# Last weights of a decode attention kernel: one head a transfer on eight semaphores, and VectorE copies the half that is finished last

## Chip, cores and metric

The kernel runs on one core of one Trainium2 chip. The metric is the device time of one execution in microseconds (us). Executions of one kernel agree within some 0.3%. Times in the profile count from the span's start. The span (439.6 us before) is shorter than the time (441.3 us), because it runs from the core's first to its last instruction.

TensorE multiplies matrices (PE, and PEld for its weight loads), VectorE is DVE, ScalarE is ACT, GpSimd is POOL, and SyncE (SP) issues nearly all DMA transfers. Engines and transfers tell each other that they are done through semaphores, counters that one raises and another waits for.

## The reference

Two attention blocks with one new token per sequence, 4 sequences, 32 query heads on 8 key/value heads of width 128. Block A attends to all 8192 cached positions, block B to the last 2048. The two results are concatenated.

```python
q = (x @ wq).reshape(B, 1, 32, 128).transpose(0, 2, 1, 3)
scores = einsum("bhqd,bhkd->bhqk", q, repeat(k_cache, 4, axis=1)) * 128 ** -0.5
p = softmax(scores)
o = einsum("bhqk,bhkd->bhqd", p, repeat(v_cache, 4, axis=1))
return o.transpose(0, 2, 1, 3).reshape(B, 1, 4096) @ wo      # block A; B the same on k, v[..., -2048:, :]
# ... out = concatenate([a, b], axis=-1)
```

## The kernel before

K and V stream through SBUF, the core's on-chip memory, in 20 units. A unit is one sequence and two K/V heads of block A (4 MB of K, 4 MB of V), or one sequence of block B. TensorE transposes K, computes scores, sums the softmax and multiplies P by V. Ten turns of two units each run as a hardware loop on TensorE. The last unit, L, ends in straight code after the loop. Its output is projected with the last 8 heads of `wo`, which have a buffer of their own, `Wl_sb` (1 MB).

```python
# TensorE, after the loop. V of unit L comes in pieces of 4, 2, 1 and 1 eighths ("VL" 0..3).
VCH = [4, 2, 1, 1]
for c in range(NC):                                  # 8 chunks of 16 P.V matmuls
    w = [("VL", vch_of[c])]
    # ...
    if c == 4:
        pe_SM(L)                                     # softmax sum: 16 matmuls of 64 columns
        op("pe", pe_seed, waits=[("ocp", NTURN - 1)])  # puts the sum so far into both halves
    pe_PV(L, c, bank=KTB[0], waits=w)
add_norm(L, bank=KTB[0])                             # VectorE scales P.V by 1/sum: OT_sb ("otr")

WCH = [3, 2, 2, 1]                                   # heads per weights transfer
for i, n in enumerate(WCH):
    for hq in range(h0, h0 + n):
        for hf in range(2):                          # halves[0] in bank SA, halves[1] in bank KT
            # matmul(out=halves[hf], lhsT=OT_sb[..., hq, :], rhs=Wl_sb[:, hq, half hf])
            op("pe", lfn, waits=[("WL", i), ("otr", L), ("oc", L - 1)],
               inc=("fin", hf) if hq == C - 1 else None)
    h0 += n
op("dve", copy halves[0] to osb, waits=[("fin", 0)], inc=("ocp", NTURN))      # cut to its core
op("act", copy halves[1] to osb, waits=[("fin", 1)], inc=("Ef",))             # cut to its core
op("act", dma(out[:, 0, H2:D], osb[:, 0, H2:D]), waits=[("Ef",)], inc=("out", 2))

# SP, behind V of unit L:
for i, n in enumerate(WCH):
    src = WO[0][last 8 heads].rearrange("(h p) n -> p h n", p=128)[:, h0:h0 + n, :]
    op("sp", dma(Wl_sb[:, h0:h0 + n, :], src), inc=("WL", i))
    h0 += n
op("sp", dma(out[:, 0, 0:H2], osb[:, 0, 0:H2]), waits=[("ocp", NTURN)], inc=("out", 0))
# SP's end:
for i in range(3):
    sem, val, _ = values[("out", i)]
    sp.wait_ge(sem, val)
```

## Time and profile before

| | |
|---|---|
| time, 3 runs before the prediction | 441.33 us (441.18 to 441.64) |
| span of the profiled run | 439.58 us |
| DMA over the span | 420 GB/s |
| last piece of V lands | 433.90 us |
| last projection matmul starts | 437.08 us |
| last output lands, span ends | 439.08 us, 439.58 us |

The page of the kernel before: busy time of the engines, then two rows of 40 slices of the span (TensorE's granted clock in tenths, mean busy share of the 16 DMA engines in tenths).

```profile
PE 366.2 (83%) x7312; PEld 338.0 (77%) x7312; DVE 210.1 (48%) x462; ACT 186.4 (42%) x184; POOL 27.8 (6%) x84
PEclk9999999999999988998899799969997999899999
DMA  8999999999999999999999999999999999999995
```

The DMA row says 9 everywhere except at the two ends: the loads bound the kernel. The granted clock is 0.96 in the mean (one slice shows 0.6), and TensorE, busy for 83% of the span, has some slack. A change to the last transfers can move only the last few microseconds.

The chain of work that ended last, cut to its end (start, us, what):

```profile
411.39 23.49 DMA Wl_sb<-in_A_wo_dram
...
434.88 0.04 issue
...
435.42 0.36 issue
...
437.39 0.37 ACT osb L708
```

The chain comes through the first weights transfer, waits 0.36 us for nothing that the profile shows in the middle of the projection, and leaves through ScalarE's copy. The same stretch as a timeline (start, us, engine, line, operation; in brackets the idle time before it; in the timelines here the rows of weight loads (PEld) are left out, except where one is read):

```profile
434.62 0.18 DVE L489 TENSOR_TENSOR OT_sb<-KT,RL 128x8 bf16<-128x8 f32 x1 [2.29 <-PE KT L325]
434.93 0.08 PEld L703 LDWEIGHTS SA<-Wl_sb,OT_sb 128*4 128x4 bf16 x1 [0.46 <-DMA Wl_sb<-in_A_wo_dram]
434.93 0.27 PE L703 MATMUL SA<-Wl_sb,OT_sb 128*4 128x256 bf16 x1 [0.34 <-DMA Wl_sb<-in_A_wo_dram]
435.04 0.27 PE L703 MATMUL KT<-Wl_sb,OT_sb 128*4 128x256 bf16 x1
435.14 0.27 PE L703 MATMUL SA<-Wl_sb,OT_sb 128*4 128x256 bf16 x1
435.77 0.27 PE L703 MATMUL KT<-Wl_sb,OT_sb 128*4 128x256 bf16 x1 [0.36 <-issue]
...
437.08 0.27 PE L703 MATMUL KT<-Wl_sb,OT_sb 128*4 128x256 bf16 x1
437.28 0.41 DVE L707 CAST osb<-SA 4x256 bf16<-4x256 f32 x1 [2.48 <-PE SA L703]
437.39 0.37 ACT L708 ACTIVATE osb<-KT 4x256 bf16<-4x256 f32 x1 [10.84 <-PE KT L703]
437.72 0.29 SPq L567 DMA_DIRECT2D out_dram<-osb  x1
437.79 0.27 ACTq L567 DMA_DIRECT2D out_dram<-osb  x1
```

L489 is the scaling, L703 the projection. Matmuls follow each other 0.11 us apart, but the fourth starts 0.63 us after the third. This gap is called the stop below. The weights transfers by size (KB each, median us from issue to landing):

```profile
Wl_sb<-in_A_wo_dram SPq DMA_DIRECT2D x2, 256.0 KB, 23.7
Wl_sb<-in_A_wo_dram SPq DMA_DIRECT2D x1, 384.0 KB, 23.5
Wl_sb<-in_A_wo_dram SPq DMA_DIRECT2D x1, 128.0 KB, 9.9
```

The landing of each transfer, read from the semaphore records of the trace: V's last piece 433.90; weights 434.88, 435.51, 436.19 and 436.51. A transfer is shared by 16 engines, and it has landed when the slowest has finished: of the last piece of V, the first engine's share landed at 431.07, the second-last at 433.31, the last at 433.90.

### The profile page before, as it was taken

Reading aid. Unit: us, or ns where it says so; the run is one execution under the profiler, and the core shown is the slowest. Engines: PE = TensorE matmul, PEld = TensorE weight load, DVE = VectorE, ACT = ScalarE, POOL = GpSimd, SP = SyncE. Lnnn points to the kernel's source line nnn. Section 1 sums busy time; section 2 is a strip of 40 time slices with the busy share of each in tenths; the row PEclk is TensorE's granted clock in tenths of the full one; section 3 lists DMA queues with packets and bytes.
Section 4 is the critical chain, followed back from the end, with each engine's and each line's share of the span. In section 5 each row is a group of like instructions: output and inputs, shape, how many; then the busy total and the mean of one; then the engine's idle time right before and its main releaser. Section 6 shows DMA issues by size and latency. Waiting matters only on the chain.

```text
span 439.6 us, 15816 instructions
## 1 busy us (share of the span) xinstructions
PE 366.2 (83%) x7312; PEld 338.0 (77%) x7312; DVE 210.1 (48%) x462; ACT 186.4 (42%) x184; POOL 27.8 (6%) x84
## 2 busy tenths in 40 slices
PE   0158998998997949895989698969878896989986
PEld 0158897997996949795979688968878795979965
DVE  0034455654663634463446346625643563556641
ACT  1004473473562615370635253434534361635630
POOL 6100000000000000000000000000100000000000
PEclk9999999999999988998899799969997999899999
DMA  8999999999999999999999999999999999999995
GB/s 338 427 413 421 418 417 421 423 441 409 444 429 436 418 438 429 429 427 429 432 438 420 433 444 422 437 432 429 413 446 435 429 430 429 432 427 411 447 403 211
DMA packets 13190, 184.77 MB, mean 420 GB/s; under 512 B 1348, under 2 KB 2424, under 8 KB 4472
## 3 DMA queue, kind: packets, MB, share of 16 engines
q1 hardware_dynamic: 13088, 184.56, 98.9%
q8 instruction: 8, 0.13, 0.1%
q14 instruction: 6, 0.05, 0.0%
q0 software_dynamic: 64, 0.02, 0.0%
q10 hardware_dynamic: 24, 0.01, 0.0%
HBM read 184.56 MB, written 0.01 MB: 420 GB/s over the span
## 4 chain that ended last, share of the span: by engine, by line
DMA 49%; PE 37%; PEld 8%; issue 3%; SPq 1%; PEldq 0%; DVE 0%; ACT 0%
DMA K_sb<-in_A_k_cache_dram 37%; PE KT L278 21%; DMA K_sb<-in_B_k_cache_dram 7%; PE OT L325 6%; DMA Wl_sb<-in_A_wo_dram 5%; PEld KT L278 3%; PE SA L309 3%; PE SB L309 3%; PE KT L387 2%; PEld OT L325 1%; SPq L567 1%; PEld SA L309 1%; PEld SB L309 1%; PE SA L337 1%; PE KT L261 0%
## 5 line engine op out<-in xcount | busy, mean ns | idle before, releaser
L278 PE MATMUL KT<-identf,K_sb 128*128 128x128 f32 x1280 | 208.4, 297 | 45.3 <-DMA K_sb<-in_A_k_cache_dram 32.9
L287 ACT ACTIVATE KT_sb<-KT 128x1024 bf16<-128x1024 bf16 x160 | 163.2, 1024 | 130.6 <-PE KT L278 130.6
L278 PEld LDWEIGHTS KT<-identf,K_sb 128*128 128x128 f32 x1280 | 147.6, 149 | 50.8 <-DMA K_sb<-in_A_k_cache_dram 34.1
L286 DVE COPY KT_sb<-KT 128x512 int32<-128x512 int32 x160 | 110.5, 690 | 121.8 <-PE KT L278 120.4
L325 PE MATMUL OT<-PT,V_sb 128*128 128x64 bf16 x2560 | 78.1, 193 | 2.1 <-DMA V_sb<-in_A_v_cache_dram 1.2
L325 PEld LDWEIGHTS OT<-PT,V_sb 128*128 128x128 bf16 x2560 | 75.9, 98 | 2.3 <-DMA V_sb<-in_A_v_cache_dram 1.3
L460 ACT ACTIVATE PT<-Dt 128x1024 bf16<-128x1024 f32 (+1 forms) x21 | 21.3, 1017 | 91.8 <-DVE Dt L449 91.8
L309 PEld LDWEIGHTS SA<-RQc,KT_sb 128*128 128x128 bf16 x1280 | 57.2, 98 | 2.5
L309 PEld LDWEIGHTS SB<-RQc,KT_sb 128*128 128x128 bf16 x1280 | 50.5, 97 | 7.9 <-issue 4.4
L309 PE MATMUL SA<-RQc,KT_sb 128*128 128x16 bf16 x1280 | 56.5, 170 | 0.0
L309 PE MATMUL SB<-RQc,KT_sb 128*128 128x16 bf16 x1280 | 52.8, 170 | 0.0
L411 DVE TENSOR_REDUCE M<-SB 128x8 f32<-128x512 f32 (+1 forms) x20 | 13.8, 692 | 50.3 <-PE SB L309 50.3
L432 POOL PARTITION_ALL_REDUCE MB<-M1m x20 | 7.7, 387 | 335.7 <-DVE M1m L425 335.7
L387 PE MATMUL KT<-Wo_sb,OL 128*4 128x512 bf16 x80 | 18.9, 379 | 0.0
L197 PE MATMUL KT<-ident,x_sb 4*128 4x4 bf16 x8 | 0.6, 170 | 19.5 <-POOL identf L529 19.5
L197 PEld LDWEIGHTS KT<-ident,x_sb 4*128 4x128 bf16 x8 | 0.4, 113 | 19.6 <-issue 19.6
L449 DVE TENSOR_TENSOR Dt<-SA,MBm 128x512 f32<-128x512 f32 x20 | 13.8, 691 | 0.7
L411 DVE TENSOR_REDUCE M<-SA 128x8 f32<-128x512 f32 (+1 forms) x20 | 13.6, 681 | 0.0
L449 DVE TENSOR_TENSOR Dt<-SB,MBm 128x512 f32<-128x512 f32 x20 | 13.6, 681 | 0.0
L337 PE MATMUL SA<-PT,onesb 128*128 128x64 bf16 x336 | 13.2, 192 | 0.0
L387 PEld LDWEIGHTS KT<-Wo_sb,OL 128*4 128x4 bf16 x80 | 6.0, 84 | 8.1
L337 PEld LDWEIGHTS SA<-PT,onesb 128*128 128x128 bf16 x336 | 11.1, 97 | 0.0
(72 smaller groups left out, 125.4 us busy)
## 6 DMA issues: line engine op xcount, KB each, us to landing
K_sb<-in_A_k_cache_dram SPq DMA_DIRECT2D x15, 4096.0 KB, 24.5
V_sb<-in_A_v_cache_dram SPq DMA_DIRECT2D x15, 4096.0 KB, 29.5
K_sb<-in_B_k_cache_dram SPq DMA_DIRECT2D x16, 1024.0 KB, 22.1
V_sb<-in_B_v_cache_dram SPq DMA_DIRECT2D x16, 1024.0 KB, 19.0
V_sb<-in_B_wq_dram SPq DMA_DIRECT2D x1, 4096.0 KB, 12.3
V_sb<-in_A_wq_dram SPq DMA_DIRECT2D x1, 4096.0 KB, 21.7
Wo_sb<-in_B_wo_dram SPq DMA_DIRECT2D x4, 1024.0 KB, 10.2
K_sb<-in_A_k_cache_dram SPq DMA_DIRECT2D x2, 2048.0 KB, 17.3
```

Of the source, the lines that this page charges most:

```text
L278: ins = pe.transpose(out=bkf[:, pi * 128:(pi + 1) * 128], in_=K_sbf[:, slot, t0:t0 + 2, :].rearrange("p t d -> p (t d)"), identity=identf[ ...
L286: return e.tensor_copy(out=KT_sb.bitcast(I32)[:, tj % NKT, :], in_=bkf.bitcast(I32)[:, :])
L287: return e.activation(out=KT_sb[:, tj % NKT, :], in_=bk[:, :], func=ACTF.Copy)
L309: ins = pe.matmul(out=stb[:, t % NTH * C:(t % NTH + 2) * C], lhsT=ktv[:, pi, :, e], rhs=RQc[:, u % 2, t // TS, e, :], start=(e == 0), stop ...
L325: ins = pe.matmul(out=otb[:, s * NW:s * NW + w], lhsT=V_sb[:, slot, t, :], rhs=PT[:, slot, t * C:t * C + w], start=(j == 0), stop=(j == n ...
L337: ins = pe.matmul(out=SA[u % 2][:, s * NW:(s + 1) * NW], lhsT=onesb[:, :], rhs=PT[:, u % 2, c0:c0 + NW], start=(i == 0), stop=(i == n - 1))
L387: ins = pe.matmul(out=bk[0:Bn, 0:D], lhsT=OL[:, i // REP, i % REP, :], rhs=Wo_sb[:, i // REP, i % REP, :], start=(i == 0), stop=(i == C - 1))
L411: return dve.tensor_reduce(out=M1[:, h * n:(h + 1) * n].rearrange("p (s h) -> p s h", h=C), in_=bank[:, :].rearrange("p (s j h) -> p s h j ...
L432: return pool.partition_all_reduce(MB[:, 0:n], M1m[:, 0:n], channels=128, reduce_op=ReduceOp.max)
L449: return dve.tensor_tensor(out=Dt[:, h * NTH * C:(h + 1) * NTH * C].rearrange("p (s j h) -> p s j h", s=Sh, h=C), in0=bank[:, :].rearrange ...
L460: return act.activation(out=PT[:, u % 2, a:b], in_=Dt[:, a:b], func=ACTF.Exp, scale=scale)
L567: return e.dma_start(out=dst, in_=src)
```

## The change

The intent is that the first head's matmul need not wait for three heads' weights, and that the half finished last goes to the engine and queue that get it out sooner. The names of four more semaphores aside, the diff is:

```diff
-        WCH = [3, 2, 2, 1]
+        WCH = [1] * C
         h0 = 0
         for i, n in enumerate(WCH):
             for hq in range(h0, h0 + n):
-                for hf in range(2):
+                for hf in (1, 0):
```

The list `WCH` is read on both sides: TensorE waits on one semaphore per head, and SP issues eight transfers of 128 KB. VectorE still copies half 0 and ScalarE half 1; the order of the matmuls decides which is finished last.

## The prediction

> **What bounds the kernel.** The DMA. The slices show it 90% or more busy nearly throughout, at 420 GB/s over the span; TensorE is 83% busy. Only the order and size of the last weights transfers change, so only the last 6 us of the 439.6 us span can move.
>
> **The tail now** (timeline and landings of the single transfers, us from the span's start). The last piece of V lands at 433.90; the last 16 P·V tiles start at 433.94. VectorE scales the result from 434.62 to 434.80. The first weights transfer (three heads) lands at 434.88, and the first projection matmul starts at 434.93: the transfer costs at most 0.08 us. Sixteen matmuls follow, 0.11 us apart; TensorE stops once, from 435.14 to 435.77, for nothing that the profile shows ("issue"; it is inside the first three heads, so no weights wait). The other transfers land at 435.51, 436.19 and 436.51; their heads start at 435.99, 436.43 and 436.86, so none is waited for. Then two copies side by side: VectorE 437.28 to 437.69 (0.41 us), ScalarE 437.39 to 437.76 (0.37 us). Their output DMAs land 1.18 us (SP's) and 1.29 us (ScalarE's) after they start, at 438.90 and 439.08. The later one ends the kernel.
>
> **What the change does.**
> 1. One head a transfer. Head 0 can land some 0.6 us earlier (estimate from 0.32 us a head on the slowest engine), so the first matmul waits for the scaling alone: at most -0.08 us. Without the stop, later heads would gain too: 0.3 us at best, since head 7 lands at 436.51 and starts at 436.86. If the stop ends at a fixed time, both gains vanish. I expect it to remain.
> 2. Four more transfers on SP, same bytes, same order. A fixed cost per transfer isn't visible: two heads take the fastest engine 0.76 us, one head 0.36 us. The Trainium skill ("DMA: Bandwidth & Descriptors", Anatomy of one DMA) calls the semaphore write itself essentially free; this trace agrees. SP's third weights issue is held 14.2 us and the fourth 2.9 us, until 429.5; descriptors in flight on the slowest engine come to some 92 at both releases, so I take that as a limit. With one more descriptor per extra transfer I estimate the last issue near 431; its data isn't due before 433.7. Off the chain.
> 3. Order of halves. ScalarE's half now ends 0.11 us before VectorE's: ScalarE's output lands at 437.28 + 0.37 + 0.03 + 1.29 = 438.97, VectorE's at 437.39 + 0.41 + 0.03 + 1.18 = 439.01. The end moves from 439.08 to 439.01: -0.07 us.
> 4. Waits ride on weight loads: no instruction added on TensorE.
>
> Sum: -0.07 us, at best -0.4; expected -0.13 us of 441.33, below the spread of the three runs (0.46 us).
>
> **Predicted: 441.2 us, range 440.7 to 441.8.** Chances: faster by over 2% 0.003, within 2% 0.992, slower by over 2% 0.005.
>
> **What would show it.** Right: last P·V start unchanged; first projection matmul within 0.1 us of the scaling's end; the stop of about 0.6 us still there; ScalarE's copy 0.11 us ahead of VectorE's; outputs landing within 0.1 us of each other. Step 2 wrong: SP's last weights issue after 433, or a late matmul waiting for weights.
>
> **What would make it wrong.** A limit on the number of transfers in flight, so that SP issues the last heads late; the unexplained stop vanishing or growing with the new code; waits on each head breaking the 0.11 us beat (seven of 0.05 us would cost 0.35 us).

## The result and the profile after

| | before | after |
|---|---|---|
| time, median of 6 runs | 441.36 us (441.18 to 441.64) | 441.06 us (441.04 to 441.46) |
| span of the profiled run | 439.58 us | 439.19 us |
| last piece of V lands | 433.90 us | 433.67 us |
| tail: from there to the span's end | 5.68 us | 5.52 us |

The ratio is 0.9995, with a 95% interval of 0.9982 to 1.0008: the two kernels can't be told apart by their times. Here and below a ratio is the mean time of one kernel's fast runs over that of the other's of the same rounds, so it is not quite the ratio of the medians quoted.

Of the 0.39 us between the two spans, 0.23 us is V's last piece landing earlier. The change touches no load before it, and in later runs of kernels with the same loads it landed anywhere from 433.70 to 434.19 us, so this is variation of the run. Only the tail, 0.16 us shorter, can belong to the change. From here on the tail is the measure.

The chain of the kernel after, cut in the same way:

```profile
410.53 18.05 DMA V_sb<-in_A_v_cache_dram
...
434.38 0.32 issue
...
435.18 0.33 issue
...
437.12 0.41 DVE osb L707
```

It no longer passes through a weights transfer. It comes from V, waits 0.32 us for the scaling and still stops inside the projection. The timeline of the same stretch:

```profile
434.41 0.18 DVE L489 TENSOR_TENSOR OT_sb<-KT,RL 128x8 bf16<-128x8 f32 x1 [2.26 <-PE KT L325]
434.66 0.08 PEld L703 LDWEIGHTS KT<-Wl_sb,OT_sb 128*4 128x4 bf16 x1 [0.41 <-issue]
434.69 0.27 PE L703 MATMUL KT<-Wl_sb,OT_sb 128*4 128x256 bf16 x1 [0.32 <-issue]
434.80 0.27 PE L703 MATMUL SA<-Wl_sb,OT_sb 128*4 128x256 bf16 x1
434.91 0.27 PE L703 MATMUL KT<-Wl_sb,OT_sb 128*4 128x256 bf16 x1
435.50 0.27 PE L703 MATMUL SA<-Wl_sb,OT_sb 128*4 128x256 bf16 x1 [0.33 <-issue]
...
436.81 0.27 PE L703 MATMUL SA<-Wl_sb,OT_sb 128*4 128x256 bf16 x1
437.01 0.37 ACT L708 ACTIVATE osb<-KT 4x256 bf16<-4x256 f32 x1 [10.10 <-PE KT L703]
437.12 0.41 DVE L707 CAST osb<-SA 4x256 bf16<-4x256 f32 x1 [2.53 <-PE SA L703]
437.42 0.27 ACTq L567 DMA_DIRECT2D out_dram<-osb  x1
437.56 0.29 SPq L567 DMA_DIRECT2D out_dram<-osb  x1
```

The fourth matmul starts 0.60 us after the third, as before. ScalarE's copy is now the first by 0.11 us, and its output is issued 0.15 us before VectorE's (SP's). The weights transfers:

```profile
Wl_sb<-in_A_wo_dram SPq DMA_DIRECT2D x8, 128.0 KB, 19.8
```

Their landings are 434.02, 434.34, 434.66, 434.94, 435.31, 435.63, 435.96 and 436.29. The last is 2.62 us after V's last piece; before, it was 2.61 us. So four more transfers made the load no longer.

The tail in four parts, with events read from the two traces:

| part of the tail | before | after |
|---|---|---|
| V landed to fourth projection matmul | 1.87 | 1.83 |
| fourth to last projection matmul | 1.31 | 1.31 |
| last matmul's start to last output landed | 2.00 | 1.96 |
| last output landed to span's end | 0.50 | 0.42 |
| sum (us; rounded) | 5.68 | 5.52 |

Half of the gain sits in the last row, where the prediction hadn't looked. The earlier first matmul gave little: 0.04 us is left of it at the fourth matmul, and even that is within what this part varies by between runs, as will be seen.

### The profile page after: what moved, and what is told of

It reads as the page before. It is cut to its first block, busy times and chain, and to the rows that moved or that the text cites. A ratio compares the mean times of both kernels' runs of the same rounds, so it can differ in the third digit from the quotient of the medians.

```text
span 439.2 us, 15810 instructions
## 1 busy us (share of the span) xinstructions
PE 364.1 (83%) x7302; PEld 337.0 (77%) x7312; DVE 210.1 (48%) x462; ACT 186.4 (42%) x184; POOL 27.8 (6%) x84
## 4 chain that ended last, share of the span: by engine, by line
DMA 48%; PE 34%; PEld 11%; issue 4%; SPq 1%; PEldq 1%; DVE 0%
DMA K_sb<-in_A_k_cache_dram 37%; PE KT L278 19%; DMA K_sb<-in_B_k_cache_dram 7%; PE OT L325 5%; PEld KT L278 5%; DMA V_sb<-in_A_v_cache_dram 4%; PE SA L309 3%; PE SB L309 3%; PEld OT L325 2%; PEld SA L309 2%; PEld SB L309 2%; PE KT L387 1%; SPq L567 1%; PE KT L325 1%; PE SA L337 1%
```

## The experiments

Eleven runs followed, all correct: nine kernels, and a repeat each of the changed kernel and of `short_sum`. Three questions were open. Which of the change's two parts gave what? What is the stop? And what limits the tail once the stop is gone? The theory at the start was that the two parts are worth some 0.05 us each, and that the stop belongs to a place in TensorE's program. The rivals were that one part does it all, and that the stop follows the long wait for the scaling wherever that lies. The table collects the measurements; the runs are told one by one below it, and `fifteen`, which is not in the table, at the end.

| run | first weight load after scaling's end | third to fourth matmul | fourth matmul after the fetch began | last matmul after V | last output after last matmul | end after last output | tail |
|---|---|---|---|---|---|---|---|
| before | 0.13 | 0.63 | 2.50 | 3.18 | 2.00 | 0.50 | 5.68 |
| after | 0.07 | 0.60 | 2.62 | 3.14 | 1.96 | 0.42 | 5.52 |
| after_again | 0.07 | 0.51 | 2.63 | 3.04 | 1.96 | 0.42 | 5.41 |
| heads_only | 0.07 | 0.56 | 2.57 | 3.08 | 2.01 | 0.50 | 5.58 |
| halves_only | 0.07 | 0.23 | 2.60 | 2.82 | 1.97 | 0.42 | 5.21 |
| one_output | 0.07 | 0.30 | 2.49 | 2.82 | 2.00 | 0.42 | 5.24 |
| end_wait | 0.14 | 0.45 | 2.49 | 3.04 | 2.00 | 0.42 | 5.46 |
| pad3p1 | 1.04 | 0.11 | (first matmul: 2.50) | 3.64 | 1.96 | 0.42 | 6.02 |
| one_transfer | 1.74 | 0.11 | no stop | 4.31 | 1.96 | 0.42 | 6.69 |
| short_sum | 0.07 | 0.11 | no stop | 2.81 | 1.96 | 0.42 | 5.19 |
| short_sum_again | 0.07 | 0.11 | no stop | 2.80 | 1.96 | 0.42 | 5.18 |
| short_sum_old | 0.11 | 0.11 | no stop | 2.85 | 2.00 | 0.50 | 5.35 |

"The fetch" is a transfer of 16,384 bytes on queue q8, which the profile marks "instruction". In every run there is exactly one between 72 us and the projection, and it takes 1.1 us (1.3 us in `fifteen`). Seven others come earlier, in the kernel before until 70.4 us. There, the first of the ten branches of TensorE's loop is at 71.9 us and the last at 428.9 us: so queue q8 is quiet while TensorE repeats its loop, and has a fetch again in the straight code behind it. (Queue q14, marked "instruction" too, carries five transfers of 8,192 bytes after 72 us, the last at 388 us.) In the kernel before it began at 433.27 us. The DMA queues of the kernel before between 432.5 and 435 us (queue and kind: packets, MB, share of 16 engines):

```profile
q1 hardware_dynamic: 736, 0.73, 87.3%
q8 instruction: 1, 0.02, 2.8%
```

The q8 line is this fetch: one packet of 0.02 MB.

### Each part of the change alone

`heads_only` splits the transfers and keeps the order of the halves:

```diff
-                for hf in (1, 0):
+                for hf in (0, 1):        # against the changed kernel
```

> Only the transfers are split (eight of one head); each head's halves stay in the old order, so ScalarE copies the half that is finished last. The measure is the tail, from the last landing of V to the span's end: 5.68 us in the kernel before, 5.52 us in the changed one. Theory (the change's two parts are worth some 0.05 us each or less): the first projection matmul's weight load starts 0.07 us after the scaling instead of 0.13 us, the stop of 0.6 us stays at the fourth matmul, tail 5.6 to 5.65 us, time 441.0 to 441.4 us. Rival A (the split does it all): tail 5.52 us. Rival B (the order does it all): tail 5.68 us, first weight load no earlier after the scaling.

It took 441.38 us (441.20 to 441.73), against 441.39 us for the kernel before; ratio 1.0001 (0.9987 to 1.0015). The first weight load did come 0.07 us after the scaling. The stop stayed, and the tail was 5.58 us, a little under the theory's 5.60 to 5.65 and above rival A's 5.52. Since the stop varies from run to run, the tail by itself doesn't refute rival A; the last two parts do: 2.01 and 0.50 us, as in the kernel before (2.00 and 0.50). The split alone doesn't do it all.

`halves_only` keeps the four transfers and turns the order:

```diff
-        WCH = [1] * C
+        WCH = [3, 2, 2, 1]               # against the changed kernel
```

> Only the order of the halves changes (VectorE's half last); the weights stay in four transfers of 3, 2, 2 and 1 heads. Theory: the first weight load waits for the three-head transfer again, some 0.13 us after the scaling where that transfer lands about 1 us after the last of V; the output issued second lands last, whichever engine issues it, and what is gained is only that VectorE's output is issued some 0.03 us sooner after the last matmul than ScalarE's was: tail 5.6 to 5.66 us. Rival A: tail 5.68 us. Rival B: tail 5.52 us. Time 441.0 to 441.4 us in either case.

It took 441.22 us (441.01 to 441.54); ratio 0.9996 (0.9983 to 1.0010). Its tail of 5.21 us fits none of the three expectations, and the first weight load came 0.07 us after the scaling rather than 0.13. V landed late in this run (434.19 us), so the scaling ended only at 435.09 us, when the three-head transfer landed too. The fetch had begun at 433.03 us. The fourth matmul came 2.60 us after it, as in the others, but that was only 1.44 us after V; the gap before it was 0.23 us. So whole tails can't be compared between runs that have the stop, but their parts can. Two parts show the change. The last output landed 1.97 us after the last matmul and the span ended 0.42 us later, as in the changed kernel and unlike `heads_only` (2.01 and 0.50 us). And one wait appeared that the split avoids: the sixth head's weight load waited until 436.46 us for the third transfer, which landed at 436.42 us. With the stop short, the two-head transfer was on the chain.

### The last 0.5 us: outputs and end waits

In all runs with two outputs, the first-issued output lands 1.17 to 1.18 us after its issue and the second 0.18 us after the first, whether SP's is issued second (0.15 us later) or ScalarE's (0.07 us later). So the end follows the first-issued output. The changed kernel gains 0.04 us here, because ScalarE's copy (0.37 us) is shorter than VectorE's (0.41 us) and now comes first. `one_output` asks whether two outputs cost their spacing, by sending both halves in one transfer from SP:

```diff
-        op("act", dma(out[:, 0, H2:D], osb[:, 0, H2:D]), waits=[("Ef",)], inc=("out", 2))
-        op("sp", dma(out[:, 0, 0:H2], osb[:, 0, 0:H2]), waits=[("ocp", NTURN)], inc=("out", 0))
+        op("sp", dma(out[:, 0, 0:D], osb[:, 0, 0:D]), waits=[("ocp", NTURN), ("Ef",)], inc=("out", 0))
```

> The changed kernel with one output transfer from SP after both copies, in place of one from ScalarE and one from SP. In all runs the first-issued output lands 1.17 to 1.18 us after its issue and the second 0.19 us after the first, whether issued 0.07 or 0.15 us after it. Theory 'queued' (the second transfer's landing is behind the first's, so two cost 0.19 us): the single one, issued 0.15 us after the first of the two was, lands 1.18 us after its issue, the tail is 0.04 us shorter (5.48 us). Rival 'each has its own latency': it lands 1.22 us after its issue, as SP's did, tail the same 5.52 us.

The time was 441.08 us (441.02 to 441.23); ratio 0.9996 (0.9981 to 1.0011). The single output landed 1.25 us after its issue, neither 1.18 nor quite 1.22, and from the last matmul to its landing it took 2.00 us, 0.04 us more than with two. One output is no gain, and both expectations missed. (Its tail of 5.24 us is short because the stop was short: 0.30 us to the fourth matmul.)

The other row is the end. SP's wait for three semaphores became two instructions in the program: the first waits for outputs 2 and 1, the second for output 0. In the kernel before, output 2 lands last; its landing wakes the first instruction, and the second runs 0.08 us later. In the changed kernel, output 0 lands last, and the second instruction is all that is left. `end_wait` is the kernel before with that order turned alone:

```diff
-            for i in range(3):
+            for i in (2, 1, 0):
                 sem, val, _ = values[("out", i)]
```

> The kernel before with one edit: SP waits for the three outputs in the reverse order at the end. From the last output's landing to the span's end it is 0.49 to 0.50 us in the runs whose last landing is waited for by SP's first end instruction (before, heads_only, short_sum_old), and 0.41 to 0.42 us in those where SP's last end instruction waits for it (the changed kernel, halves_only, short_sum, one_output). Theory (the order of the end waits is part of what the swap of the halves gains): SP's last instruction now waits for ScalarE's output, which lands last; from landing to end 0.41 to 0.42 us with nothing else changed, output landings still 0.18 to 0.19 us apart. Rival (it depends on which queue lands last): still 0.49 to 0.50 us. The time moves by 0.1 us or less, too little for the interval.

From the last landing to the span's end it took 0.42 us instead of 0.50, with the outputs landing 0.18 us apart as before. So the order of the end waits accounts for 0.08 us of the tail. Its time was 441.11 us (440.63 to 441.28) against 441.58 us, ratio 0.9988 (0.9974 to 1.0001), so the times don't tell the two apart, as expected.

### The grain of the weights transfers at its worst

`one_transfer` loads all eight heads in one:

```diff
-        WCH = [1] * C
+        WCH = [C]
```

> The last output weights in one transfer of eight heads, the order of halves as in the changed kernel. Theory (the grain of the weights transfers is on the chain only through the head whose matmul waits for a landing): all 16 matmuls wait for the last landing, some 2.6 us after the last of V, then run for 1.75 us plus the stop: tail 7.0 to 7.7 us, time 442.5 to 443.3 us. Rival (the weights transfers are hidden behind something else): tail 5.5 to 5.7 us, time 441.1 us.

The time was 442.59 us (442.43 to 442.71), ratio 1.0027 (1.0012 to 1.0042): slower, clear of noise but far below 2%. The transfer landed at 436.64 us, 2.63 us after V. The scaling and the first matmul in its timeline:

```profile
434.77 0.18 DVE L489 TENSOR_TENSOR OT_sb<-KT,RL 128x8 bf16<-128x8 f32 x1 [2.26 <-PE KT L325]
436.69 0.27 PE L703 MATMUL KT<-Wl_sb,OT_sb 128*4 128x256 bf16 x1 [1.96 <-DMA Wl_sb<-in_A_wo_dram]
```

The matmul waited 1.96 us, and the row names the weights. The tail was 6.69 us, below the expected 7.0 to 7.7, because there was no stop at all. That miss is telling. The fetch had begun at 433.28 us, so instructions that come 2.5 us later were there at about 435.8 us, before the weights were. A stop that followed a long wait would have come here first of all.

### What the stop is

`pad3p1` is the changed kernel with seven more instructions on TensorE: three matmuls (two instructions each) into a free bank, and one semaphore increment. They run right after the loop, while V is awaited (the diff is shortened).

```diff
+        def pe_pad(pe):
+            for _ in range(3):
+                ins = pe.matmul(out=OTB[:, 0:64], lhsT=ident[:, :], rhs=onesb[:, 0:64], start=True, stop=True)
+            return ins
+        op("pe", pe_pad, waits=[("otr", L - 1)])
+        op("pe", lambda pe: pe.sem_inc(sems["spare"], 1))
         for c in range(NC):
```

> The changed kernel with three matmuls (into a free bank) and one semaphore instruction added on TensorE after the loop, while it waits for V, so they take no time of their own. They move the projection seven instructions on in TensorE's program. Theory 'place' (the stop of 0.6 us belongs to a place in the program, as where new instructions must be fetched): it comes seven instructions earlier by the projection's count, while TensorE waits for the scaling anyway; the sixteen matmuls run without a stop or wait only for landings; tail 5.1 to 5.3 us, time 0.2 to 0.4 us below the changed kernel's. Theory 'restart' (the stop follows the third matmul after any long wait): stop still before the fourth projection matmul, tail 5.5 us. Theory 'time' (it ends at a fixed time): also unchanged.

The scaling and the projection in its timeline:

```profile
434.78 0.18 DVE L489 TENSOR_TENSOR OT_sb<-KT,RL 128x8 bf16<-128x8 f32 x1 [2.26 <-PE KT L325]
435.99 0.08 PEld L711 LDWEIGHTS KT<-Wl_sb,OT_sb 128*4 128x4 bf16 x1 [1.37 <-issue]
436.02 0.27 PE L711 MATMUL KT<-Wl_sb,OT_sb 128*4 128x256 bf16 x1 [1.28 <-issue]
436.13 0.27 PE L711 MATMUL SA<-Wl_sb,OT_sb 128*4 128x256 bf16 x1
436.24 0.27 PE L711 MATMUL KT<-Wl_sb,OT_sb 128*4 128x256 bf16 x1
...
437.65 0.27 PE L711 MATMUL SA<-Wl_sb,OT_sb 128*4 128x256 bf16 x1
```

The sixteen matmuls now run without a stop, but between the scaling's end and the first weight load lie 1.04 us instead of 0.07: the stop has moved by the three matmuls, as the theory of a place said. In the trace it has moved by exactly seven instructions: the first late one is TensorE's semaphore wait directly before that weight load, which is seven instructions ahead of the fourth weight load. It ran at 435.91 us, though the scaling had ended at 434.95; in the changed kernel it had begun to wait at 433.79. The stop wasn't hidden, as the theory had hoped. The time was 442.02 us (441.88 to 442.09), ratio 1.0012 (0.9999 to 1.0026), and the tail 6.02 us. The first matmul started 2.50 us after this run's fetch began, and that was late: 0.49 us before V landed, against 0.79 us in the changed kernel. So 0.29 us of the 0.50 us by which this tail is longer than the changed kernel's 5.52 comes with the fetch, and about 0.2 us with the new place of the stop. So two things hold together. Which instruction waits is fixed by its place in the program. When it may run is fixed by the fetch, 2.49 to 2.63 us after its transfer began in all eight runs with a stop. The length of the stop is only what is left of that time: from the third to the fourth matmul it took 0.23 to 0.63 us, where 0.11 us is normal.

The Trainium skill ("Runtime: NRT & Kernel Launch", Instruction fetch mechanics) says that each engine's instructions are refilled in blocks of 16 KiB, which are 256 instructions, and that crossing a block's edge is mostly hidden. The block size agrees with the 16,384-byte transfer in the trace. That the cost is hidden doesn't hold here. The trace doesn't name the engine that a fetch is for; that it is TensorE's follows from the stop moving with TensorE's program alone. The traces add that the fetch goes with TensorE's progress: it begins 0.24 to 0.82 us after the second half of the last unit's P.V matmuls has begun, in `fifteen` too, where these matmuls and the fetch (434.87 us, against 432.83 to 433.52 us in the others) were late.

`short_sum` moves the edge the other way. The last softmax sum takes 2 matmuls of 512 columns instead of 16 of 64 with the same result, so the projection comes 28 instructions earlier in the program and the edge should fall behind its 32 (the diff is shortened):

```diff
+        def pe_SM_last(u):
+            def fn(pe):
+                for i in range(2):
+                    ins = pe.matmul(out=SA[u % 2][:, 0:512], lhsT=onesb[:, :], rhs=PT[:, u % 2, i * 512:(i + 1) * 512],
+                                    start=(i == 0), stop=(i == 1))
+                return ins
+            op("pe", fn, waits=[("exp", u)], inc=("SM", u))
-                pe_SM(L)
+                pe_SM_last(L)
# and in dve_sum, for the last unit, 512 columns are reduced instead of 256
```

> The changed kernel, with the last softmax sum on TensorE as 2 matmuls of 512 columns instead of 16 of 64 (28 instructions fewer, some 0.1 us less TensorE time before the last P.V tiles, while V is still awaited). In every run so far the stop ended 2.5 to 2.6 us after an instruction-fetch transfer of 16 KB began, and seven more instructions before the projection moved the stop from its fourth matmul to ahead of its first. Theory (a block of instructions begins at the projection's fourth matmul; it arrives late): with 28 fewer, the block begins behind the projection's last matmul, no stop is left in it, the heads follow their landings; last matmul 2.8 to 2.95 us after V's last landing instead of 3.14, tail 5.1 to 5.3 us (5.52 before), time some 0.2 to 0.4 us below the changed kernel's: 440.7 to 441.0 us. Rival (the stop comes with the long wait for the scaling, the padded run's move was chance): stop still in the row, tail 5.4 to 5.6 us.

The scaling, the first, third and fourth matmul, and the weight loads of the last two heads in its timeline:

```profile
434.59 0.18 DVE L499 TENSOR_TENSOR OT_sb<-KT,RL 128x8 bf16<-128x8 f32 x1 [2.00 <-PE KT L325]
434.87 0.27 PE L713 MATMUL KT<-Wl_sb,OT_sb 128*4 128x256 bf16 x1 [0.32 <-issue]
...
435.08 0.27 PE L713 MATMUL KT<-Wl_sb,OT_sb 128*4 128x256 bf16 x1
435.19 0.27 PE L713 MATMUL SA<-Wl_sb,OT_sb 128*4 128x256 bf16 x1
...
436.24 0.08 PEld L713 LDWEIGHTS KT<-Wl_sb,OT_sb 128*4 128x4 bf16 x1 [0.20 <-DMA Wl_sb<-in_A_wo_dram]
...
436.56 0.08 PEld L713 LDWEIGHTS KT<-Wl_sb,OT_sb 128*4 128x4 bf16 x1 [0.24 <-DMA Wl_sb<-in_A_wo_dram]
...
436.67 0.27 PE L713 MATMUL SA<-Wl_sb,OT_sb 128*4 128x256 bf16 x1
```

The stop is gone, and the last two heads wait for their weights (0.20 and 0.24 us on the weight load's row), 0.04 us after these land at 436.20 and 436.52 us. The tail is 5.19 us, as expected. The time is 440.69 us (440.62 to 440.87) against 441.17 us, ratio 0.9986 (0.9973 to 1.0000).

`short_sum_old` applies the same edit to the kernel before, to see what the change is worth without the stop:

> The same shorter sum in the kernel before (four weights transfers, old order of halves). Theory: without the stop the weights transfers are on the chain, and there the split is worth more than it was with the stop: the two-head transfer lands some 2.3 us after V's last, its two heads and the last one follow, last matmul 2.85 to 3.0 us after V's last landing, tail 5.3 to 5.5 us, that is 0.1 to 0.25 us above the split kernel with the short sum. Rival (the grain doesn't matter): the same tail as that kernel within 0.05 us, plus 0.04 us for the order of halves.

The time is 440.81 us (440.65 to 441.03), ratio 0.9989 (0.9975 to 1.0002), and the tail 5.35 us. Against `short_sum` that is 0.16 us: 0.04 us up to the last matmul, because the sixth head waits for a two-head transfer (landed 436.20, head started at 436.24), 0.04 us in the outputs and 0.08 us in the end waits. That is within the theory's 0.1 to 0.25 us, above the 0.09 us that the rival allowed, but by luck: half of it is the end waits, which neither had counted. The finer grain of the transfers is worth only 0.04 us even here, which is within the rival's 0.05; the rest belongs to the order of the halves.

The changed kernel and `short_sum` then ran once more in one call:

> The changed kernel once more, beside the next one on the same chip: 441.0 to 441.4 us, tail from V's last landing 5.2 to 5.6 us, the stop there, its end 2.4 to 2.7 us after the instruction fetch began.

> The changed kernel with the short sum once more: 440.6 to 440.9 us, no stop among the projection's first ten matmuls, tail 5.15 to 5.25 us, the last heads 0.03 to 0.06 us after their landings; faster than the changed kernel of the same call by 0.2 to 0.5 us. If the first run's gain was the chip's or the run's, the two agree within 0.15 us.

They took 441.19 us (440.87 to 441.29; ratio 0.9990, 0.9977 to 1.0004) and 440.68 us (440.61 to 441.16; ratio 0.9982, 0.9969 to 0.9996), with 441.58 us for the kernel before. The tails were 5.41 and 5.18 us. Against the changed kernel the tail of `short_sum` is 0.23 us shorter, and its median time is 0.5 us lower; no interval was taken for that pair, and one of the five runs of `short_sum` (441.16 us) lies among the changed kernel's. Its lead over the kernel before is small, but in the repeat its interval lies clear of one.

### A failed attempt on the slow engine

The tail begins when the slowest of 16 DMA engines has finished V, and the last heads follow that engine. The Trainium skill ("DMA: Bandwidth & Descriptors", Why a DMA increments its semaphore by 16 and not by 1) says that a transfer uses the largest number of engines up to 16 that divides its rows, the lowest-numbered ones. `fifteen` is `short_sum` with V's last two pieces and the eight weights transfers each cut into 8 and 120 partitions, so that the highest-numbered engine would be left out of the larger part:

```diff
-                op("sp", dma(Wl_sb[:, h0:h0 + n, :], src), inc=("WL", i))
+                for p0, p1 in ((120, 128), (0, 120)):        # both on the same semaphore
+                    part(Wl_sb[p0:p1, h0:h0 + n, :], src[p0:p1], ...)
# and the same for the last two pieces of V
```

> The changed kernel with the short sum, where the last two V pieces and the eight weights transfers are each split into 8 and 120 partitions. [...] The Trainium skill (DMA: Bandwidth & Descriptors, Why a DMA increments its semaphore by 16) says that a 120-partition transfer uses the lowest-numbered 15 engines and an 8-partition one the lowest 8. Theory A (the late engine is the highest-numbered): last V piece lands 0.3 to 0.7 us earlier relative to the one 1 MB before it, weights 0.3 us or more earlier. Theory B (it is another): V's last landing is unchanged or up to 0.3 us later, for the engines carry 1/15 more. The time of the whole moves by less than 0.5 us either way.

It took 445.71 us (444.23 to 446.25), ratio 1.0089 (1.0070 to 1.0107), far outside the 0.5 us that was allowed for. Two windows of `short_sum` (us, busy us and count of PE, PEld, DVE, ACT and POOL, granted clock, DMA share, GB/s):

```profile
428.00:432.00 4.00, 2.81 (x69) 2.15 (x70) 1.19 (x4) 0.00 (x0) 0.20 (x1) 1.00 1.01 399
432.00:436.00 4.00, 3.69 (x78) 2.89 (x77) 0.73 (x3) 0.00 (x0) 0.00 (x0) 1.00 0.71 237
```

The same two windows of `fifteen`:

```profile
428.00:432.00 4.00, 2.53 (x76) 2.10 (x72) 0.95 (x3) 0.00 (x0) 0.20 (x1) 1.00 0.94 235
432.00:436.00 4.00, 2.82 (x37) 1.77 (x36) 0.90 (x2) 0.00 (x0) 0.00 (x0) 0.81 0.99 241
```

The rate fell from 399 to 235 GB/s in the first window, while the engines stayed busy (0.94), and in the second the granted clock fell to 0.81. (In `short_sum` the loads were nearly over in that window, so its 237 GB/s there tells nothing.) Even the undivided piece of V ahead of them landed at 434.17 us instead of 431.28. The semaphore records agree with the skill's rule on the number of engines: each divided piece shows 23 landings, 8 and 15. Which engine is the slow one isn't told for certain. But each of the eight weights pairs has two landings, 0.18 to 0.22 us apart, that come some 1.0 us behind the other 21. An engine that carries both parts would give that, and the highest-numbered engine carries neither, so it speaks against theory A. Neither theory had a place for the slowness. Why the divided transfers ran so slowly is open.

## Why the prediction was right, and which of its steps were not

The predicted time was 441.2 us (440.7 to 441.8), and 441.06 us was measured; "within 2%" was right. It was right for its main reason: the loads set when the tail begins, and the change touches only the tail. But the range is 1.1 us wide, and a prediction of no change at all would have been right as well; only the steps are put to a test.

1. **Head 0 lands earlier: at most -0.08 us, and it vanishes if the stop ends at a fixed time.** Right. Head 0 landed 0.35 us after V instead of 0.99, and the first load came 0.06 us sooner after the scaling (0.13 to 0.07 us). `heads_only`, `pad3p1` and `one_transfer` show that the stop's end follows the fetch, so nothing of it need be left behind the stop. Without the stop, the split was worth 0.04 us, well below the 0.3 us called the best case.
2. **Four more transfers, off the chain.** Right in effect: the weights landed 2.62 us after V, as before (2.61), and the fastest engine took 0.33 to 0.38 us a head. (The section of the skill that this step names describes transfers issued from GpSimd; these are SP's.) The reason given was not right. SP's last five issues were held 3.2, 6.5, 2.9, 1.8 and 1.0 us; the last ended at 429.29 us, not near 431. Counting descriptors in flight on the slowest engine in the same way at the ends of these issues (an estimate from the rows of the transfers and their landings) gives figures that rise from some 79 to some 97, so the limit of 92 was a chance agreement of two points.
3. **Order of halves: -0.07 us.** The size came out at -0.04 us in the landings. The mis-sized term was the output's latency, taken as 1.29 us for ScalarE's and 1.18 us for SP's. It goes with the order of issue, not the engine: the first lands after 1.17 to 1.18 us, the second 0.18 us later. So the expected 0.04 us between the two landings was 0.18 us. A second term was missing altogether: 0.08 us from the order of SP's end waits, shown by `end_wait`. Together they are 0.12 us.
4. **No instruction added on TensorE.** Right, and of more weight than thought: with seven added instructions the tail of `pad3p1` was 0.5 us longer, some 0.2 us of it by the place of the stop.

The expected sum was -0.13 us and the tail lost 0.16 us (0.27 us in the repeat), partly by other terms than named: that the two numbers are so near is luck. The rest of the 0.30 us between the medians is not told apart from run-to-run variation. What stays open: what exactly sets the moment at which the fetch begins (0.49 to 1.16 us before V's landing, 2.89 us in `fifteen`), why instructions run only 2.5 us later, what limits SP's transfers in flight, and why `fifteen` was slow.

## What to carry to other kernels

When a kernel is bound by its loads up to the last microseconds, list the tail's events from the last landing to the span's end and change only what the next event waits for; finer transfers paid 0.04 us here, because other waits ended later. A gap called "issue" that keeps its place in the program may be instructions that arrive late: look for a fetch transfer a few microseconds earlier, and move the code across it, preferably by making the code shorter. For differences far below the spread of the times, compare distances between events, and check in several runs of one kernel which of these distances are steady.

## What the Trainium skill lacked or had wrong

- "Runtime: NRT & Kernel Launch", Instruction fetch mechanics: it calls crossing a 16 KiB block mostly hidden. The section excepts taken branches, and this stretch follows a loop, whose last branch came 3.75 to 5.43 us before the fetch; whether that plays a part no run tests. In this tail it cost between 0.1 and 1.0 us over the normal spacing, and the instructions behind the edge ran 2.49 to 2.63 us after the fetch transfer began, though the transfer itself took 1.1 us. The page has no figure for that.
- "DMA: Bandwidth & Descriptors", Rules for kernel authors: it advises coalescing small transfers and finds mostly overhead under 64 KB, but says nothing of pieces queued behind a long load. Eight transfers of 128 KB behind a full queue ended 2.62 us after V's last piece, and four of up to 384 KB ended after 2.61 us, so coalescing gained nothing here, and one transfer of 1 MB cost 1.2 us of time (442.59 against 441.39 us for the kernel before).
- The same page, Why a DMA increments its semaphore by 16 and not by 1: it tells how many engines 120 and 8 partitions get (15 and 8, as the landings here confirm), but gives no rate for such a split. Here the rate fell from 399 to 235 GB/s, for a reason that stays open.
- No page that was read has the spacing of two small outputs issued closely (0.18 us between landings, at 0.07 and at 0.15 us between issues), or the 0.08 us that the order of the final waits costs.
